# A recurrent attention fed into a PReLU network: one hand-written order of instructions replaced by another

## Chip, cores and metric

The kernel runs on one core of a Trainium2 chip. The metric is the device time of one execution in microseconds (us), as the median of several. The engines are TensorE (PE; its weight loads are listed as PEld), VectorE (DVE), ScalarE (ACT) and GpSimd (POOL); SyncE (SP) issues transfers (DMA), and ACT and POOL issue some too.

## The reference

Four batches of eight heads have 768 positions of 48 numbers. A recurrence gives y, which is laid out as 3072 tokens of 384 numbers and passed through a network with 2048 hidden units:

```python
f = 1.0 / (1.0 + np.exp(-f_logit))
state = np.zeros((B, H, D, D))
for t in range(S):
    state = f[:, :, t, :, None] * state + np.einsum('bhd,bhe->bhde', k[:, :, t], v[:, :, t])
    y[:, :, t] = np.einsum('bhd,bhde->bhe', q[:, :, t], state)
x = y.transpose(0, 2, 1, 3).reshape(B * S, H * D)
h = x @ w_in
g = np.maximum(h, 0.0) + alpha * np.minimum(h, 0.0)
return g @ w_out
```

## The kernel before

**Steps.** The sequence is cut into 6 chunks of 128 positions, and the batches into 2 pairs. This makes 12 steps, numbered 0 to 11, each of 256 tokens. A step has an attention part, whose result is a tile xT (384 x 256), and a network part, which turns xT into 256 rows of the output.

**Attention part.** It loads f, q, k, v (L313, L323; by SP in step 0 and by POOL in the others), takes the sigmoid (ACT), and forms products of decays on DVE (L338, L373 to L406, L440). PE then runs small products, mostly 48 x 32 weights, 64 instructions to a group: raw (L582) for lags of 0 to 3 positions, qu (L591) for lags inside a block of 32, off (L566) between blocks. DVE picks from them what counts (L599, L451) into a tile ad, ACT places that in A (L606), and PE multiplies with v and the state (py, L614), whose result ACT copies out (L494, in steps 0 and 1 L729). The keys are turned, by PE (pk, L713) in steps 0 and 1 and through DRAM (SP, L473 and L475) later, and the increments of the state (pd, L539, 64 products) are added by DVE (L550, L554). The result y goes to DRAM and back into xT by SP (L503, L505), or token by token (L626) in steps 1 and 11, or over PE (L738) in step 0.

**Network part.** Layer 1 makes eight pieces ph of the hidden units (L831). A piece is 6 products in full float32 (each two records), or, for pieces 3 to 6 from step 3 on, three passes in a faster form: xh with hi, xl with lo, xs with sum. xl and xs come from an accumulating DMA that POOL issues (L823). ACT makes the negative part (relu, L854), DVE two products that make the gate (L859). Layer 2 of step 0 is a plain product (po, L866). From step 1 on, it is seven block products in the manner of Strassen (pa twice, pc, pb, pd, pe, pf; L886, 16 records each), for which DVE adds halves of the gate (L880, eight per step, named m, u, v, w) and combines the results (L896, ACT L921); SP stores them (L765).

**Weights.** w_in and w_out come as float64 words, in eight pieces each of about 767 KB (L277, SP), and are cut to float32 by two ACT operations (L281, L282) and one of DVE (L291). That runs beside the first two steps. Fourteen idle products (L935) stand at the start of PE's work, six more before the first small products, and eight behind them.

**What sets the order.** `ORDER_WORDS` names every part of the work once, for instance `0u1` (step 0, qu of batch 1) or `3Na5` (network of step 3, layer-1 piece 5). Letters used below: e loads, G the two scans (L373, L374), r raw, u qu, o off, d increments, y py (of batch 0 or 1 of the pair, the two halves of one PSUM tile), Y the copy of py out of PSUM (ACT, L494, L729), I and J the filling products of step 0, K the way of the keys, X the way of y into xT; in networks a, b the products of a piece, r and c its relu and gate, p0 to p6 the block products (pa, pc, pb, pa, pd, pe, pf), u, v, w, m the sums, s the stores; without a step's number a and w are the two halves of converting a w_in piece, b and v those of w_out. The loop at the end (L947 to L959) calls the parts in the order of the words, and each engine under the manual schedule gets its instructions in that order. Those engines are PE, DVE and ACT; what SP and POOL issue is ordered by the framework.

Of the kernel before, what the change touches and what calls it, by code (L numbers as in the profile page):

```python
# [18 lines left out]
C = 128  # L19
# [22 lines left out]
0e 1e 0I0 0f 0F 0G 0g 0r1 0h 0i 0m 0p 0j 0r0 0I1 0l 0I2 a0 0R0 0I3 0I4 0I5 0q 0o a1 0k a2 0O 0s 0t w0 0u0 0U0 0R1  # L42
0K0 0H0 1f 0J0 0J1 0J2 w1 0K1 0u1 0J3 0U1 1F 0A0 0d 0D 0H1 0A1 w2 1G 0J4 0J5 0y0 0Y0 b0 0J6 0y1 0x0 0Y1 0M 1g 1i 0J7
1r0 0x1 1R0 0X a3 1h a4 b1 w3 a5 1m 1r1 w4 1j 0Na0 v0 0Nr0 0Na1 0Na2 1R1 0Na3 a6 0Nc0 w5 0Nr1 0Na4 0Na5 0Nc1 2e 0Nr2
1l 1k 0Nr3 a7 0Nc2 1o b2 0Nr4 1K0 1p 1O v1 w6 w7 0Na7 1K1 0Nc3 0Nc4 b3 v2 b4 0Na6 1q 0Nr5 0Nc5 1u0 0Nr6 b5 0Nc6 0Nr7
v3 1u1 1s 2f 1U0 0Nc7 b6 1U1 1H0 1A0 2F 1t 0Np0 v4 0Np1 0Np2 v5 1d b7 v6 V 1H1 1D v7 2g 0Np3 0Np4 1A1 1y0 1y1 1Y0
0Np5 W0 1Y1 1X W1 Y3 W2 0Np6 W3 2G 1Na0 W4 W5 0Np7 0No0 2h 1M 0No1 2i 1Nr0 1Na1 Y4 Y5 1Na3 2p 1Nr1 2q W6 1Na2 1Na4
Y6 3e 1Nr2 2u0 2l 1Nc0 1Nr3 2t 1Nc1 2k 1Nm0 1Nr4 1Nc2 2r0 1Nc3 W7 1Nm1 1Na5 1Nc4 1Na6 1Nr5 2R0 1Nr6 2r1 2U0 2K Z3
2u1 1Nc6 2R1 2A0 1Na7 1Nr7 1Nc5 2o 1Np0 2U1 2O 3f 1Nc7 2d Z4 1Nk 2D 2A1 1Np2 3F 1Np1 2y0 2y1 1Np3 2Y0 2Y1 2X 1Nu0
1Nu1 1Nv0 3G 3g 1Np4 1Nd 1Nv1 1Nw0 1Ng 2M 1Nw1 1Ne 1Nj 1Nh 1Np5 3h 1Np6 1Nf 1Nl 3p 1Ni 3i 1NL 2Na0 3l 4e 2Nr0 2Na1  # L50
2Nr1 2Na3 2Na2 1Ns1 3q 2Nr2 3r0 3u0 2Nc0 2Nr3 3k 3t 2Nc1 2Nm0 3R0 3U0 2Na5 2Nc2 2Nc3 2Nm1 2Na4 Z5 2Nr4 3r1 2Nr5 3K
3u1 2Na7 3R1 2Na6 3o 3A0 2Nc5 2Nr6 2Nc4 3O 3U1 2Nc6 Z6 3A1 3d 3D 2Np0 2Nr7 2Np1 2Nk 2Nc7 4f 2Nd T 3y0 3y1 4F 3Y0
2Np2 1Ns0 3Y1 3M 4g 2Np3 4r0 2Nu1 2Nu0 2Np4 3X 2Nv0 4G 2Nv1 2Nw0 2Ng 3Nx 3Ny 2Nw1 2Ne 2Nj 2Nh 2Np5 4h 2Np6 2Nf 2Nl
4p 3Na1 3Nz 3Na0 4i 3Nr0 2NL 2Ni 4k 4l 3NY 3Na2 4q 3Nr1 3Na7 4K 3Na3 5e 2Ns1 3Nr2 3Nc0 3NZ 3Na4 3Nc2 4t 3Nc1 3Nr7
3Nm0 4u0 3Nc7 4R0 4U0 3Nq3 3Na6 4r1 4A0 4R1 3Na5 4u1 4U1 3Nq4 3Nq5 3Nq6 4o 4O 3Nb3 3Nr3 3Nc3 3Nb4 3Nm1 2Ns0 3Nb6
3Nb5 4d 3Nr4 3Nr5 4D 3Np0 4A1 3Nr6 3Nc6 3Nc5 4y0 3Nc4 4y1 3Np2 5f 4M 4Y0 4Y1 3Np1 3Nk 5F 4X 5g 3Np3 3Nu0 3Nu1 3Nv0
5G 3Nv1 3Nw0 3Ng 3Np4 4Nx 4Ny 3Nw1 3Nd 3Ne 5h 3Nj 3Np5 3Np6 3Nh 3Nf 3Nl 5p 3Ni 5r0 4Nz 4Na0 5i 4Nr0 4Na1 3NL 5k 4NY
4Na5 5l 4Nq5 4Na2 5q 4Nr1 5K 4Na3 4Nc0 4Nr2 5u0 5t 4Nc1 4Nm0 4Nc2 5R0 5U0 4Na7 4Nr7 4NZ 4Na4 6e 3Ns1 5r1 4Nc7 4Nq4
4Nq3 5A0 5u1 5R1 5U1 4Na6 4Nb5 4Nb3 5o 4Nq6 4Nr3 5d 5O 4Nc3 4Nb4 5A1 4Nm1 5D 4Nr4 4Nr5 4Nb6 4Np0 4Nr6 5y0 4Nc4 4Nc5
6f 4Nc6 5y1 5Y0 6F 4Np2 5Y1 5X 6g 4Nk 4Np1 4Np3 4Nu0 4Nu1 4Nv0 4Nv1 4Ng 6G 5Nx 5M 4Nw0 4Np4 5Ny 4Nw1 4Nd 3Ns0 4Ne 6h  # L60
4Nj 4Nh 4Np5 4Nf 4Nl 6p 4Ni 5Nz 5Na0 4Np6 6i 5NY 6k 5Nr0 5Na1 4NL 6l 5Na2 6q 5Na7 5Nr1 6t 5Nc1 6u0 5Nr2 5Nc0 6r0
5Nm0 5Nc2 6R0 5Nr7 5NZ 7e 4Ns1 5Na4 6K 5Na3 6U0 5Nc7 5Na5 6r1 5Nq3 6A0 6u1 6R1 6U1 5Nq4 5Nb3 5Nq5 5Na6 5Nb4 6o 5Nr3
5Nq6 5Nc3 6O 6A1 6d 5Nm1 5Nb6 6D 5Nb5 5Nr4 5Nr5 5Np0 5Nr6 5Nc4 5Nc6 7f 6y0 5Nc5 5Nk 7F 6y1 6Y0 5Np2 6Y1 5Np1 6X 7g
5Np3 5Nu0 5Ng 7G 5Nu1 5Nv0 5Nv1 5Nw1 5Np4 6Nx 5Nw0 5Nd 6M 5Ne 6Ny 7h 5Nj 5Nh 5Np5 5Nf 5Np6 4Ns0 7p 5Ni 6Nz 6Na0 5Nl
7i 7l 6NY 6Nr0 6Na1 5NL 7k 7q 6Na2 6Nr1 7t 6Nc1 6Nr2 6Nc0 6Na7 6Nm0 7K 6Na3 6Nq3 7r0 6Nc2 7u0 7R0 6Nr7 6NZ 6Na4 8e
5Ns1 7U0 6Nc7 6Nq4 6Na5 7u1 7r1 6Nq5 7A0 7R1 7U1 6Na6 6Nq6 6Nb3 6Nr3 6Nc3 6Nb4 6Nm1 6Nb6 6Nb5 7A1 7o 6Nr4 6Nr5 6Nc4
6Nr6 7d 8f 6Np0 7O 6Nc5 7D 6Nk 6Np1 7y0 8F 7y1 6Nc6 7Y0 6Np2 7Y1 7X 8g 7Nx 7M 6Np3 6Nu0 6Nu1 6Np4 6Nv0 6Nd 6Nv1 6Nw0
6Ng 8G 7Ny 6Ne 6Nj 6Nw1 8h 6Nh 6Np5 6Nf 7NY 6Np6 5Ns0 6Nl 8p 6Ni 8i 7Nz 7Na0 7Nr0 7Na1 7Nr1 6NL 8k 8l 7Na2 8t 8r0
7Nr2 7Nc0 8q 7Nc1 8R0 9e 6Ns1 8K 7Na3 7Nm0 7Na7 8u0 7Nc2 7Nr7 7NZ 7Na4 8U0 7Na5 7Nq3 7Nq4 7Nc7 8r1 8u1 7Nq5 8A0 7Na6
8R1 7Nb4 7Nb3 8U1 7Nq6 7Nr3 7Nc3 7Nm1 7Nb6 7Nb5 8o 8A1 8d 7Nr4 7Nr5 7Nc4 7Nr6 8D 8O 9f 7Np0 7Nc5 7Nk 7Np1 7Nc6 8y0  # L70
9F 8y1 8Y0 8Y1 7Np2 8X 9g 7Nd 8M 7Np3 7Nu0 7Nu1 8Nx 7Ne 7Np4 7Nv1 7Ng 9G 8Ny 7Nv0 7Nw0 7Nw1 7Np5 7Nh 9h 7Nf 7Nj 9r0
7Np6 6Ns0 7Nl 9p 7Ni 9R0 8Nz 8Na0 8Na7 9i 8Nr0 8Na1 7NL 9k 9l 8Na2 9q 8Nr1 8NY 8Nr2 9t 8Nc0 8Nc2 8Nc1 8Nr7 8NZ 8Na4
10e 7Ns1 8Nm0 9u0 9U0 9K 8Na3 8Na5 8Nq4 9A0 8Nq3 9u1 9r1 8Na6 8Nc7 9R1 9U1 8Nq5 8Nq6 8Nb3 8Nb4 8Nr3 8Nc3 8Nm1 8Nb6
8Nb5 8Nr5 9o 8Nr4 8Nc5 9A1 8Nr6 9O 9d 8Np0 8Nc4 9D 8Nk 8Np1 8Nc6 10f 9y0 9y1 8Np2 10F 9Y0 9Y1 9X 10g 9M 8Np3 8Nu0
8Nu1 10r0 8Np4 8Nd 9Nx 8Nv0 8Nv1 8Nw0 8Ng 10G 8Np5 8Ne 8Nw1 9Nz 10h 9Ny 8Nh 8Nj 8Nf 10p 8Np6 7Ns0 8Nl 8Ni 9NY 9Na0
# [21 lines left out]
ORDER = flat()  # L97


@with_exitstack  # L100
def kernel(
# [147 lines left out]
    def load_weights(dst, src, name):  # L249
# [25 lines left out]
        def upper(n):  # L275
            raw = stage.tile([128, WP, 4], I16, tag="raw", name=f"{name}_raw{n}", bufs=RAWS)
            nc.sync.dma_start(out=raw.rearrange("p (a n) four -> p a (n four)", a=rows_)[:, :, 0:4 * width - 1],  # L277
                              in_=words[:, :, 4 * n * width + 1:4 * (n + 1) * width])

            lead = stage.tile([128, WP], F16, tag="lead", name=f"{name}_lead{n}", bufs=LEADS)  # L280
            nc.scalar.activation(lead, raw[:, :, 2].bitcast(BF16), AF.Copy, scale=0.5)  # L281
            nc.scalar.activation(as_int(n, I32), by_row(raw.bitcast(U32)[:, :, 0]), AF.Copy, scale=2.0 ** -13)  # L282
            got[n] = lead
# [21 lines left out]
    def loaded(bp, c, x):  # L305

        i = f"{bp}_{c}"
        b0 = U * bp
        loads = nc.gpsimd if bp or c else nc.sync

        def load(name, src):
            t = work.tile([128, W], F32, tag=name, name=f"{name}_{i}", bufs=1)
            loads.dma_start(out=t.rearrange("p (u x) -> p u x", u=U),  # L313
                              in_=src[b0:b0 + U, c].rearrange("u p h t -> p u (h t)"))
            return t

        x["kt"] = load("f", fT)
        f = x["f"] = quads(x["kt"])
        q = x["q"] = load("q", qT)
        x["k"] = load("k", kT)  # L320
        for cc in range(NC2):
            t_, _ = halves(cc)
            loads.dma_start(out=vs[bp][t_, cc, :, 0:DM], in_=v[b0:b0 + U, c, t_].rearrange("u t d -> t u d"))  # L323

    def lagging(bp, c, x):
        f, q = x["f"], x["q"]
        x["k4"] = work.tile([128, W], F32, tag="k4", name=f"k4_{bp}_{c}", bufs=1)
        kr = quads(x["k4"])
        nc.scalar.activation(f, f, AF.Sigmoid)
        nc.scalar.copy(kr[:, :, 2:3], f[:, :, 3:4])  # L330
        nc.scalar.copy(qd[:, :, 0:DB], q.rearrange("p (g t) -> p g t", t=DB))

    def lagged_all(bp, c, x):
# [7 lines left out]
        nc.vector.tensor_tensor(kr[:, :, 1:2], f[:, :, 2:3], f[:, :, 3:4], ALU.mult)  # L341
        lagged(1)
        nc.vector.tensor_tensor(kr[:, :, 0:1], f[:, :, 1:2], kr[:, :, 1:2], ALU.mult)
        lagged(2)
# [670 lines left out]
```

## Time and profile before

| what | value |
|---|---|
| median of 3 runs | 595.64 us (595.24 to 597.02) |
| span of the profiled execution | 592.1 us (592.08) |
| time of the profiled execution itself | not recorded apart from its span |
| instructions | 18,853 |
| first layer-1 product to last block product | 42.70 to 588.62 us |
| k, q, f loads from step 1 on | 512 KB each, 4.2 to 5.2 us to landing |
| weight pieces | 16 of about 767 KB, 9.5 us to landing |

The span goes from the first to the last record of the profile; the median is 3.56 us longer. An engine's busy time is the time in which one of its instructions runs. A wait is idle time of an engine ahead of an instruction, put down to what released it; "issue" means that the profile shows nothing that was waited for. The granted clock is the share of its full speed that PE got.

### The profile page before, as it was taken

Reading aid. Unit: us, or ns where it says so; the run is one execution under the profiler, and the core shown is the slowest. Engines: PE = TensorE matmul, PEld = TensorE weight load, DVE = VectorE, ACT = ScalarE, POOL = GpSimd, SP = SyncE. Lnnn points to the kernel's source line nnn. Section 1 sums busy time; section 2 is a strip of 40 time slices with the busy share of each in tenths; the row PEclk is TensorE's granted clock in tenths of the full one; section 3 lists DMA queues with packets and bytes.
Section 4 is the critical chain, followed back from the end, with each engine's and each line's share of the span. In section 5 each row is a group of like instructions: output and inputs, shape, how many; then the busy total and the mean of one; then the engine's idle time right before and its main releaser. Section 6 shows DMA issues by size and latency. Waiting matters only on the chain.

```text
span 592.1 us, 18853 instructions
## 1 busy us (share of the span) xinstructions
PE 580.1 (98%) x8200; PEld 527.9 (89%) x8200; DVE 505.7 (85%) x1027; ACT 300.4 (51%) x561; POOL 68.4 (12%) x114
## 2 busy tenths in 40 slices
PE   8799999999999999999999999999999999999997
PEld 6678767899899999999999999899899999899997
DVE  7889799899999989899989889989989979966243
ACT  5697973461472473483382374374275355443230
POOL 9110010000101101111111101101100100100100
PEclk9689999999999999999999999999999999999999
DMA  9959212612523823724624614722732731611300
GB/s 299 356 160 348 98 22 63 172 30 86 123 86 91 191 78 89 172 65 105 169 60 106 153 68 106 164 74 85 148 110 81 152 110 54 112 44 30 80 2 27
DMA packets 69443, 67.57 MB, mean 114 GB/s; under 512 B 44688, under 2 KB 58640, under 8 KB 69360
## 3 DMA queue, kind: packets, MB, share of 16 engines
q1 hardware_dynamic: 59744, 37.16, 22.1%
q0 software_dynamic: 8880, 28.84, 19.2%
q8 instruction: 64, 1.05, 0.7%
q10 hardware_dynamic: 736, 0.37, 0.2%
q14 instruction: 19, 0.16, 0.1%
HBM read 44.99 MB, written 13.50 MB: 99 GB/s over the span
## 4 chain that ended last, share of the span: by engine, by line
PE 80%; issue 10%; DMA 4%; ACT 3%; DVE 3%; POOL 1%; POOLq 0%; ACTq 0%; DVEq 0%
PE ph L831 36%; PE pa L886 9%; PE pd L886 5%; PE pf L886 5%; PE pe L886 5%; PE pb L886 5%; PE pc L886 4%; PE py L614 3%; PE qu L591 3%; PE raw L582 3%; DMA w_out_raw<-in_w_out 2%; PE pd L539 1%; PE off L566 1%; DVE ad L451 1%; DMA f<-in_fT 1%
## 5 line engine op out<-in xcount | busy, mean ns | idle before, releaser
L831 PE MATMUL ph<-xT,w_in_sb 128*128 128x256 f32 x612 | 137.1, 380 | 0.2 <-DMA xT<-y 0.2
L831 PEld LDWEIGHTS ph<-xT,w_in_sb 128*128 128x128 f32 x612 | 115.1, 190 | 16.9 <-issue 0.9
L854 ACT ACTIVATE gate<-ph 128x512 f32<-128x512 f32 x96 | 54.6, 594 | 134.4 <-PE ph L831 127.5
L859 DVE SCALAR_TENSOR_TENSOR gate<-gate,om,ph 128x256 f32<-128x256 f32 x192 | 81.0, 476 | 25.6 <-ACT gate L854 25.1
L886 PE MATMUL pa<-w_out_sb,gate 128*128 128x192 f32 x352 | 61.7, 329 | 0.0
L880 DVE TENSOR_TENSOR gate<-gate 128x512 f32<-128x512 f32 x88 | 57.6, 690 | 3.2 <-PE pb L886 2.4
L886 PEld LDWEIGHTS pa<-w_out_sb,gate 128*128 128x128 f32 x352 | 57.1, 190 | 0.5
L599 DVE COPY_PREDICATED ad<-mraw,raw 128x256 f32<-128x256 int32 (+1 forms) x96 | 42.7, 445 | 8.9 <-PE raw L582 6.2
L451 DVE COPY_PREDICATED ad<-mquad,qu 128x224 f32<-128x224 int32 (+6 forms) x140 | 42.2, 302 | 6.8 <-PE qu L591 1.7
L606 ACT COPY A<-ad 32x256 f32<-32x256 f32 x96 | 38.7, 403 | 11.8 <-DVE ad L451 10.4
L440 DVE TENSOR_TENSOR scores<-scores,fs 128x768 f32<-128x768 f32 (+5 forms) x60 | 37.4, 623 | 1.6
L844 ACT ACTIVATE ph<-ph 128x512 f32<-128x512 f32 x36 | 20.2, 574 | 34.0 <-PE ph L831 25.2
L831 PE MATMUL ph<-xh,hi 128*128 128x256 f32 x216 | 34.4, 295 | 0.0
L831 PE MATMUL ph<-xl,lo 128*128 128x256 f32 x216 | 32.0, 283 | 0.3 <-issue 0.3
L886 PE MATMUL pb<-t,gate 128*128 128x192 f32 x176 | 31.2, 331 | 0.0
L831 PEld LDWEIGHTS ph<-xh,hi 128*128 128x128 f32 x216 | 28.7, 190 | 2.8 <-issue 1.6
L424 ACT COPY A<-q 48x512 f32<-48x512 f32 x44 | 27.2, 617 | 7.8 <-DVE q L398 7.2
L886 PE MATMUL pd<-t,gate 128*128 128x192 f32 x176 | 30.7, 328 | 0.3 <-DVE gate L880 0.3
L886 PE MATMUL pc<-t,gate 128*128 128x192 f32 x176 | 30.6, 327 | 0.0
L886 PE MATMUL pf<-w_out_sb,gate 128*128 128x192 f32 x176 | 30.5, 327 | 0.0
L323 POOL DMA_DIRECT2D vs<-in_v x22 | 13.2, 605 | 149.4 <-PE py L614 149.1
L886 PE MATMUL pe<-w_out_sb,gate 128*128 128x192 f32 x176 | 30.4, 326 | 0.0
(153 smaller groups left out, 1044.0 us busy)
## 6 DMA issues: line engine op xcount, KB each, us to landing
w_out_raw<-in_w_out SPq DMA_DIRECT2D x8, 767.8 KB, 9.6
w_in_raw<-in_w_in SPq DMA_DIRECT2D x8, 767.2 KB, 9.5
q<-in_qT POOLq DMA_DIRECT2D x11, 512.0 KB, 5.1
f<-in_fT POOLq DMA_DIRECT2D x11, 512.0 KB, 5.2
k<-in_kT POOLq DMA_DIRECT2D x11, 512.0 KB, 4.2
turned<-f SPq DMA_DIRECT2D x40, 128.0 KB, 4.4
ksn<-turned SPq DMA_DIRECT2D x10, 512.0 KB, 3.5
out<-o SPq DMA_DIRECT2D x24, 192.0 KB, 1.9
```

Source lines behind the costliest of these rows:

```text
L424: nc.scalar.copy(A[halves(cc)[1], :, par * HP:(par + 1) * HP, CH * cc:CH * (cc + 1)], x["q3"][rows(par)].rearrange("p (u h c) s t -> p u h ...
L440: nc.vector.tensor_tensor(by_four(us[:, :, UO[m]:UO[m] + 4 * n]), by_four(us[:, :, skip:skip + 4 * n]), spread(fq[:, :, 1:1 + n], n), ALU. ...
L451: nc.vector.copy_predicated(ad[:, u, :, :, 4 * m:DB], mquad[:, lo:lo + n].bitcast(I32).unsqueeze(1).unsqueeze(1).broadcast_to((128, 2, HP, ...
L582: nc.tensor.matmul(raw[DB * j:DB * (j + 1), par, hp * C:hp * C + QW], lhsT=x["k"][r_, g * DB:(g + 1) * DB], rhs=qd[r_, g], start=True, sto ...
L599: nc.vector.copy_predicated(adu[:, :, :, d:4], mraw[:, d, :, d:4].bitcast(I32).unsqueeze(1).broadcast_to((128, H, NB, n)), rv[:, :, QO[d]: ...
L606: nc.scalar.copy(A[s_, u, :, s_], ad[s_, u].rearrange("p r h t -> p (r h) t"))
L831: nc.tensor.matmul(banks[f][:, j * T:(j + 1) * T], lhsT=of[:, kt, 128 * j:128 * (j + 1)], rhs=by[:, kt], start=first_ and kt + j == 0, sto ...
L844: nc.scalar.activation(banks[f], banks[f], AF.Copy, scale=1.0 - 1.0 / EPS)
L854: nc.scalar.activation(to, of, AF.Relu, scale=-1.0)
L859: nc.vector.scalar_tensor_tensor(to[:, j], to[:, j], om[:, m:m + 1], of[:, j], ALU.mult, ALU.add)
L880: nc.vector.tensor_tensor(block(to)[:, p], block(x_)[:, p], block(y_)[:, p], op)
L886: nc.tensor.matmul(banks[to][:, 0:DH], lhsT=block(of)[:, f], rhs=of_w_out(by)[:, f], start=start and f == 0, stop=f == NH - 1, skip_group_ ...
```

## The change

The words become finer and are put in another order, for all engines. Each part becomes a generator that stops (`yield`) after an instruction or a group, and each occurrence of its word runs it to the next stop. So one part can be spread: `0F 0F 0F a1 1ev 0ek` runs three instructions of F, then a stage of a weight piece, then two loads. The word e is split into ef, eq, ek, ev. POOL and SP are put under the manual order, so the place of a word sets when their transfers are issued as well. Tiles that more than one part needs are made at first use (`Later`). The instructions are the same; a tile pd_ is renamed inc_. The lines move: py to L717, ph to L944, the block products to L1002, the gate to L968 and L975, the sums to L996.

```diff
+class Later(dict):
+    def __init__(self):
+        self.make = {}
+    def __missing__(self, key):
+        self[key] = self.make[key]()
+        return self[key]
...
+class Word:
+    def __init__(self, part):
+        self.part, self.left = part, None
+    def __call__(self):
+        if self.left is None:
+            got = self.part()
+            self.left = got if hasattr(got, "gi_frame") else iter(())
+        next(self.left, None)
...
         def whole(f):
             banks[f] = bank(f"ph{f}_{i}")
             if by_parts(f):
                 products(f, late["hi"][:, f - SPLIT[0]], late["xh"], True, False)
+                yield
                 products(f, late["lo"][:, f - SPLIT[0]], late["xl"], False, False)
...
-    with tc.manual_schedule(engines={mybir.EngineType.PE, mybir.EngineType.DVE, mybir.EngineType.Activation}):
+    with tc.manual_schedule(engines={mybir.EngineType.PE, mybir.EngineType.DVE, mybir.EngineType.Activation,
+                                     mybir.EngineType.Pool, mybir.EngineType.SP}):
...
+        run = {key: Word(part) for key, part in run.items()}
         for key in ORDER:
             run[key]()
```

Some stretches of the words, as they were and as they are (the ends of step 1's and step 2's attention, and the last block products of step 9's network):

```diff
-1A1 1y0 1y1 1Y0 0Np5 W0 1Y1 1X W1 Y3 W2
+1A1 1A0 1A0 1A0 1A0 1y1 1Y1 1y0 1Y0 1X 1X 1X
...
-2y0 2y1 1Np3 2Y0 2Y1 2X
+2y1 2Y1 1Nu0 1Nv0 3h 2y0 2Y0 2X 2X
...
-9Np2 10y0 10M 9Nd 10y1 10Y0 10Y1 9Np3 9Ng 11G 10X 11g 9Nu1 9Nu0 9Nv0 9Np4 9Nv1 9Nw0 9Np5
+9Np2 9Nu0 10Y1 10Y0 11q 11R0 9Nm1 11q 9Np3 11h 11u0 11R0 11G 11i 11i 11i 11r1 11k 10X 10X 10X 9Nv0 11l 9Np1 11U0 9Nu1 9Nd 11U0 9Nv1 11k 11K 9Np4 9Np5 9Nw0
```

More of the change, by code (lines that the diff above doesn't have):

```diff
@@ L47 @@
[L47 to L51, printed above, removed]
@@ L315, in load, with f_, q_, k_ @@
             return t
[L317 to L323, printed above, removed]
+        def f_():
+            x["kt"] = load("f", fT)
+            x["f"] = quads(x["kt"])
+        def q_():
+            x["q"] = load("q", qT)
+        def k_():
+            x["k"] = load("k", kT)
+        def v_():
+            for cc in range(NC2):
+                t_, _ = halves(cc)
+                loads.dma_start(out=vs[bp][t_, cc, :, 0:DM], in_=v[b0:b0 + U, c, t_].rearrange("u t d -> t u d"))
+                if not cc:
+                    yield
+        return {"ef": f_, "eq": q_, "ek": k_, "ev": v_}
     def lagging(bp, c, x):
-        f, q = x["f"], x["q"]
+        f = x["f"]
         x["k4"] = work.tile([128, W], F32, tag="k4", name=f"k4_{bp}_{c}", bufs=1)
@@ L466, in fifth @@
             carried(x)
+            yield
             nc.vector.transpose(x["kt"], x["ks"].rearrange("p g s t -> p (g s t)"))
         def keys():
-            ksn = x["ksn"] = work.tile([128, U, HP * 128], F32, tag="ksn", name=f"ksn_{i}", bufs=1)
+            ksn = x["ksn"]
             way = dram.tile([128, W], F32, tag="turned", name=f"turned_{i}", bufs=2)
@@ L486, in out_ @@
         def out_(u):
-            if not u:
-                x["py"] = pair(f"py_{i}")
             summed(x["py"], bp, u)
         def kept_out(u):
-            if not u:
-                x["y"] = work.tile([128, HP, U, C], F32, tag="ksn", name=f"y_{i}", bufs=1)
             nc.scalar.copy(x["y"][:, :, u], x["py"][:, u].rearrange("p (h t) -> p h t", h=HP))
@@ L633, in opening @@
         i = f"{bp}_{c}"
+        ahead(bp, c, x)
         def two(name):
@@ L716, in kept_keys @@
         def kept_keys(u):
-            if not u:
-                x["ksn"] = work.tile([128, U, HP * 128], F32, tag="ksn", name=f"ksn_{i}", bufs=1)
             nc.scalar.copy(x["ksn"][:, u], x["pk"][u])
         def out_(u):
-            if not u:
-                x["py"] = pair(f"py_{i}")
             summed(x["py"], bp, u)
         def kept_out(u):
-            if not u:
-                x["y"] = work.tile([128, HP, U, C], F32, tag="ksn", name=f"y_{i}", bufs=1)
             nc.scalar.copy(x["y"][:, :, u], x["py"][:, u].rearrange("p (h t) -> p h t", h=HP))
         def dense_(u):
-            if not u:
-                x["xt"] = [bank(f"xt{kt}_{i}") for kt in range(NK)]
             for kt in range(NK):
@@ L956 @@
                 run.update({(f"J{k}", 0): lambda x=x: idled(x["off"][0], 256) for k in range(BEHIND)})
-        assert sorted(run, key=str) == sorted(ORDER, key=str), (set(run) ^ set(ORDER), len(ORDER) - len(set(ORDER)))
+        assert set(run) == set(ORDER), set(run) ^ set(ORDER)
+        run = {key: Word(part) for key, part in run.items()}
         for key in ORDER:
             run[key]()
+        assert all(word.ended() for word in run.values()), [key for key, word in run.items() if not word.ended()]
 def _level_masks():
```

232 lines of the change are left out of this document (164 added, 68 removed).

## The prediction

> **What bounds the kernel now.** First the page's span and busy times, then its slices:
>
> ```profile
> span 592.1 us, 18853 instructions
> ...
> PE 580.1 (98%) x8200; PEld 527.9 (89%) x8200; DVE 505.7 (85%) x1027; ACT 300.4 (51%) x561; POOL 68.4 (12%) x114
> ...
> PEclk9689999999999999999999999999999999999999
> ```
>
> TensorE (PE) is the bound; its granted clock dips in the second slice alone. The windows view gives stretches (length, busy time of PE, PEld, DVE, ACT, POOL, granted clock, DMA share, GB/s):
>
> ```profile
> 15.50:19.00 3.50, 0.99 (x66) 0.91 (x67) 3.44 (x9) 2.90 (x6) 1.89 (x3) 0.99 1.01 391
> 19.00:33.00 14.00, 14.00 (x244) 11.15 (x242) 11.51 (x26) 9.15 (x20) 0.73 (x1) 0.51 1.01 334
> 43.00:589.00 546.00, 543.99 (x7504) 498.58 (x7502) 471.25 (x966) 269.33 (x503) 50.47 (x69) 1.00 0.39 101
> ```
>
> The first layer-1 product (ph) starts at 42.70 us, the last block product ends at 588.62. From 43 to 589 PE idles 2.0 us. So an order of the same instructions can win little after 43 us, and whatever wait it adds to PE is lost one for one. The waits view from 42 to 593 us (total, times, longest) names what there is to win:
>
> ```profile
> PE off L566 <- issue: 0.7, 1, 0.7
> PE ph L831 <- issue: 0.3, 1, 0.3
> PE pd L886 <- DVE gate L880: 0.3, 1, 0.3
> PE ph L831 <- DMA xT<-y: 0.2, 1, 0.2
> ```
>
> Two have no data behind them: "issue". The DMA view from 206 to 209 us, around the larger (packets, MB, share of 16 engines):
>
> ```profile
> q0 software_dynamic: 158, 0.58, 75.2%
> q8 instruction: 1, 0.02, 2.0%
> ```
>
> q8 is PE's own code: the page has 64 packets of it, 1.05 MB, so 16 KB each, and 16,400 PE records over 64 packets are 256 instructions each. In the trace this packet ran from 206.25 to 207.21, while a k load held q0, and PE went on at 208.66, 1.45 us later. At the other wait the packet ended at 342.27 and PE went on at 343.70, 1.43 us later. Both times PE had just run small products, which use up code fastest (64 qu and 64 off last 1.7 us).
>
> **The change part by part.** Both kernels have the same instructions. Only orders change, SP's and POOL's included. I followed the new orders with their semaphore waits and added row durations between each wait and what releases it.
>
> (1) Small products apart. A packet starts 1.1 to 1.5 us after PE comes within 64 instructions of the block before it, 3.3 to 5.5 us beside a load; with 1.0 us of packet and 1.43 behind, 320 instructions must last about 3.7 us, or 5.6 beside a load. After the first ph ten such stretches of the old order are under 5.6 (the two that waited: 4.78 and 5.54), two of the new (5.27 and 5.38). Gain: 0.69 idle, and 0.61 at 343.70, where an xl group took 1.33 instead of 0.72: **-1.3** (ends -1.3 and 0).
>
> [...]
>
> (2) Time behind transfers. At 90.91 step 1's network waits for xT; twelve products take 3.33 us with the wait, 2.59 elsewhere. Between py of step 1 and its first ph lie 5.4 us of PE work in the old order, 12.5 in the new, and in no step under 11.6; the longest such transfers in the trace take 8 to 10. **-0.74.** xl and xs keep 20.1 and 26.1 us of cover, against 16.3 and 21.4 needed: nothing.
>
> (3) pd at 498.37 waits for DVE, where two scans (1.3 us) stand ahead of the sums; 16 products take 3.17 instead of 2.60. In the new order a second block product lies between pb and pd. **-0.57.**
>
> (4) The first large product behind small ones takes 2.80 us for 16, others 2.60. Such returns fall from 51 to 48: 3 x 0.20, **-0.6**; the sums of all PE rows (542.76 and 542.16) give the same.
>
> (5) The readout of py. py of the two batches are halves of one tile. In the new order the words of steps 1, 2, 4, 6, 7 and 8 read `1y1 1Y1 1y0`: the first half is copied out (Y, ACT) ahead of the other half's products (y), and PE's order then has a wait on ACT in front of these. In the old order both y come first (`1y0 1y1 1Y0`), except in step 0, whose price the timeline shows:
>
> ```profile
> 34.10 1.15 PE L614 MATMUL py<-A,vs 128*64 128x64 f32 x32 [0.78 <-ACT ad L688]
> 35.19 0.70 PE L935 MATMUL off_0a<-ones 128*128 128x256 f32 x2
> 35.78 0.58 ACT L729 COPY y<-py 128x512 f32<-128x512 f32 x1
> ...
> 36.42 1.15 PE L614 MATMUL py<-A,vs 128*64 128x64 f32 x32 [0.54 <-ACT y L729]
> ```
>
> The second group starts 0.06 us after the copy ends and had waited, with two filling products between. In the six steps PE has nothing between. With ACT free: 0.16 until a reader follows PE's last product, 0.59 of copy (0.587 in its row), 0.05 on: 0.80. 6 x 0.80, **+4.8**; in step 7 ACT has part of a relu ahead, **+0.3**. Ends: 0, if PE really waits for nothing there, and 9, if ACT has one relu (0.59) ahead each time.
>
> (6) DVE's lateness. DVE gets faster by the new order: in the trace a DVE instruction that needs the result of the one just ahead starts 0.034 us after its end, any other 0.083 before it; such direct successors fall from 316 to 187, 129 x 0.117 = 15 us. That doesn't shorten PE, and PE's waits on DVE stand closer: at the first qu of step 6 PE has one ph piece and pf (2.59 + 2.60) since the last gate it needed, DVE a combination (0.35), score products (some 2.6), three operations on the state (0.95, 0.55, 0.55), a raw copy (0.44) and gaps until the pair of banks is free: 5.7, late by 0.5. The same in step 5; six places more are late by 0.05 to 0.15 each, where ph or qu waits for a bank. Also pb directly behind the last ph in steps 1 and 2: its gate is ready 1.3 and 1.8 us after PE leaves ph (0.16, relu 0.59, DVE 0.48 twice), pb reads it at 1.95 and 2.27: nothing. **+1.8.** Ends: 0 and 7.6, one sum (0.69) late in each of 11 networks.
>
> (7) The start. pk (at 18.77) comes at about 15.9 by its rows, but the k load of step 0 stands behind a weight piece on SP, and more conversions lie ahead on ACT; the sums put the first ph 0.5 us later than the old order's. Then a ph piece waits 0.8 for a bank that DVE reads behind weight sums, and the increments of step 1 wait 1.7 for ACT's copy of the keys behind weight conversions. Together 3.0; weight landings (9.5 us in the median, 6 to 20 in the trace) may move all of it. **+2.0**; ends -2.7, the clock not halved, and +4.
>
> (8) SP's and POOL's other moved transfers are covered by 11 us and more of PE work (the two stores of network 0 ahead of the keys' way back: 25). The tail keeps its copy, store and 3.46 us. Nothing.
>
> Sum: 592.08 of the profiled span plus 3.56 around it is the median 595.64. 595.64 - 1.3 - 0.74 - 0.57 - 0.6 + 4.8 + 0.3 + 1.8 + 2.0 = **601.3**: slower. The same sums along the old order find its wait at pd and no other of over 0.1 from DVE or ACT.
>
> **The rivals.**
> (a) Only the readouts count: DVE and the start give nothing away. 592.43 + 4.8 = 597.2, at the bound of "no change". For: DVE's 15 us. Against: the chains of (6) and (7).
> (b) The other side: the six readouts cost nothing, because the waits are met when PE gets there. 592.4 with nothing lost elsewhere. It decides from 0.23 us per readout, above which the gain is under 0.3%. For: no such wait is seen after 42 us in the old kernel. Against: step 0's row.
> (c) DVE becomes the bound. It is busy 471 of 546 us; one more sum late per network makes (6) 7.6: 607.1.
> (d) The pause of PE near 15 us gets too short to halve the clock. In the trace PE was busy 0.99 of 3.50 us, then got 0.51 for 14.00 us of unbroken work; without that the first ph comes 2.7 earlier: 596.6 to 598.6. [...]
>
> **How the numbers follow.** 0.3% is 1.8 us, about what a measurement of this kernel can tell from no change. Forecast 0.52 (598.6 to 604; the fetch rule's 602.6 lies in it), (a) 0.13, (b) 0.08, (c) 0.17, (d) 0.10. Faster: (b) but for its upper edge, 0.07. Same (593.85 to 597.4): half of (a), half of (d) and the rest of (b), 0.13. Slower: 0.80. The range leaves out (b) and the far end of (c): 596.5 to 606.
>
> **What would show it.** PE's waits: py on ACT y (L717) six times, some 0.8 each; qu on DVE at steps 5 and 6; none for issue beside a k load, for xT, for pd. ph's first start near 43.2, with the clock row's second slice telling of (d). If PE doesn't wait at py, the sign is wrong; if waits on the gate (L975, L996) sum to over 5 us, it is (c).

## The result and the profile after

The kernel after takes **613.09 us** in the median of 4 runs (612.14 to 614.59); the kernel before, run beside it, 595.44 us (593.93 to 597.02, 4 runs). The ratio is 1.0299, with a 95% interval of 1.0274 to 1.0323. The forecast was 601.3 us: the sign was right, and of the 17.65 us lost only 5.66 were foreseen. The profiled execution took 612.78 us, with a span of 610.4. Its page has, in the rows known from before:

```profile
span 610.4 us, 18819 instructions
...
PE 586.5 (96%) x8200; PEld 531.0 (87%) x8200; DVE 493.6 (81%) x1027; ACT 303.3 (50%) x561; POOL 66.8 (11%) x114
...
PEclk9679999999999999999999999999999999999999
```

The same 8200 matmul records take 6.4 us longer, and DVE got 12.1 us faster (15 were forecast), which did not shorten PE's time. PE is still the bound, now with pauses. PE's ten largest waits from 43 to 612 us (total, times, longest):

```profile
PE py L717 <- ACT y L587: 3.6, 5, 0.9
PE ph L944 <- issue: 2.7, 3, 1.3
PE inc L633 <- ACT ad L802: 1.5, 1, 1.5
PE py L717 <- ACT A L709: 1.0, 2, 0.5
PE inc L633 <- ACT A L672: 1.0, 1, 1.0
PE py L717 <- ACT y L839: 0.7, 1, 0.7
PE qu L690 <- DVE scores L530: 0.5, 1, 0.5
PE qu L690 <- issue: 0.4, 1, 0.4
PE ph L944 <- DVE f L504: 0.4, 1, 0.4
PE qu L690 <- DVE ad L543: 0.3, 1, 0.3
```

Six of them are the readouts of py (five on L587, one on L839), as forecast. xT and pd are gone, as forecast. "Issue" wasn't to appear beside a load, and is here four times. The 1.5 ahead of inc (the increments, pd_ before) stands where (7) forecast 1.7; the 1.0, in step 7, was not forecast. The start is in the windows (length, busy time of PE, PEld, DVE, ACT, POOL, granted clock, DMA share, GB/s):

```profile
15.50:19.00 3.50, 1.92 (x72) 1.50 (x72) 3.47 (x10) 2.58 (x5) 1.89 (x3) 1.00 0.89 297
19.00:33.00 14.00, 12.49 (x234) 9.55 (x235) 6.76 (x19) 9.33 (x22) 1.73 (x3) 0.53 1.02 309
...
36.80:40.20 3.40, 3.40 (x25) 2.98 (x22) 3.16 (x5) 2.83 (x7) 0.00 (x0) 0.50 0.01 2
...
74.50:78.00 3.50, 3.50 (x68) 2.62 (x69) 3.41 (x8) 3.44 (x5) 0.00 (x0) 0.53 0.02 5
```

Before, the clock was halved once, from 18.9 to 32.6 us. Now it is halved there, although PE was busy for 1.92 of the 3.5 us ahead (0.99 before), and again at 36.8 and at 74.3. The first ph starts at 45.64 us instead of 42.70.

**Where the time went.** Up to the first ph 2.94 us are lost. Behind it I laid each group of PE beside the usual duration of such a group, its row. What is beyond the rows (a pause, and the slower products next to it) sums to 2.3 us in the kernel before and 18.4 after; the rows themselves sum to 0.6 less in the new order. 2.94 + 18.4 - 2.3 - 0.6 = 18.4, and the spans differ by 18.3. The 18.4 are: readouts 6.3 (five of 0.90 and 1.80 in step 7), waits for issue 4.5, the stretch from the first ph to 80 us 3.1, qu waiting for DVE in steps 5 and 6 1.2 (0.80 of it idle), inc of step 7 waiting for ACT 1.2, and 2.1 in small pieces. These shares shift by up to about 1 us with the duration that is taken as usual; the idle times and the total do not.

One readout, in step 2, in the timelines of PE and of ACT (start, duration, what, idle time before and its releaser):

```profile
135.06 1.15 PE L717 MATMUL py<-A,vs 128*64 128x64 f32 x32
136.90 1.15 PE L717 MATMUL py<-A,vs 128*64 128x64 f32 x32 [0.69 <-ACT y L587]
```

```profile
136.26 0.59 ACT L587 COPY y<-py 128x512 f32<-128x512 f32 x1 [2.56 <-PE py L717]
```

ACT had been idle for 2.56 us, so the copy starts as soon as the first half is there, and PE's second half starts 0.05 us behind the copy's end. This is the row of step 0 again, without filling products in between.

One wait for issue, in PE's timeline, and the DMA queues around its packet (packets, MB, share of 16 engines):

```profile
205.85 1.08 PE L690 MATMUL qu<-scores,k 48*32 48x112 f32 x64
206.91 0.91 PE L681 MATMUL raw<-qd,k 48*32 48x80 f32 x64
207.75 0.98 PE L944 MATMUL ph<-xh,hi 128*128 128x256 f32 x6
208.57 0.40 PE L944 MATMUL ph<-xl,lo 128*128 128x256 f32 x2
210.14 0.74 PE L944 MATMUL ph<-xl,lo 128*128 128x256 f32 x4 [1.18 <-issue]
```

```profile
q1 hardware_dynamic: 4132, 0.52, 71.8%
q0 software_dynamic: 21, 0.09, 19.6%
q8 instruction: 1, 0.02, 1.1%
```

Two small groups, qu and raw, stand end to end in the *new* order, although the change is meant to keep them apart; PE stops eight products of a large piece later, while its code (q8) shares the engines with 4132 small packets on q1. I counted PE's instructions in blocks of 256 and put beside each stop the packet that brings the block. Every stop comes at the same place of a block, to within one instruction (number 193 to 195 of 256, counted from PE's first record):

| kernel | PE within 64 instructions of the block before | packet | its end + 1.43 | PE goes on |
|---|---|---|---|---|
| before | 202.89 | 206.25 to 207.21 | 208.64 | 208.66 |
| after | 158.83 | 165.84 to 166.80 | 168.23 | 168.25 |
| after | 200.58 | 207.62 to 208.50 | 209.93 | 210.14 |
| after | 445.34 | 449.02 to 449.94 | 451.37 | 451.34 |
| after | 492.00 | 495.77 to 496.83 | 498.26 | 498.11 |

All four stops end within 0.21 us of their packet's end + 1.43, as the forecast has it. The packets start 7.01, 7.03, 3.68 and 3.78 us behind the second column, against 3.36 before: the two long stops have very late packets; the two short ones have packets about as late as before, and stretches of small products that end before 6 us.

### The profile page after: what moved, and what is told of

The parts are those of the page before. It is cut to its first block, busy times and chain, and to the rows that moved or that the text cites. A ratio compares the mean times of both kernels' runs of the same rounds, so it can differ in the third digit from the quotient of the medians.

```text
span 610.4 us, 18819 instructions
## 1 busy us (share of the span) xinstructions
PE 586.5 (96%) x8200; PEld 531.0 (87%) x8200; DVE 493.6 (81%) x1027; ACT 303.3 (50%) x561; POOL 66.8 (11%) x114
## 3 DMA queue, kind: packets, MB, share of 16 engines
q0 software_dynamic: 8880, 28.84, 18.3%
q8 instruction: 64, 1.05, 0.7%
## 4 chain that ended last, share of the span: by engine, by line
PE 63%; DVE 18%; ACT 7%; DMA 5%; issue 3%; SPq 1%; POOL 0%; DVEq 0%; ACTq 0%; POOLq 0%
PE ph L944 26%; PE pa L1002 7%; PE pb L1002 4%; PE pf L1002 3%; PE py L717 3%; PE pd L1002 3%; PE qu L690 3%; PE pc L1002 3%; PE pe L1002 3%; PE po L982 2%; DVE scores L530 2%; PE raw L681 2%; DVE ad L700 2%; DMA f<-in_fT 1%; DVE gate L996 1%
## 5 line engine op out<-in xcount | busy, mean ns | idle before, releaser
L944 PE MATMUL ph<-xT,w_in_sb 128*128 128x256 f32 x612 | 141.1, 382 | 1.6 <-issue 1.3
L944 PEld LDWEIGHTS ph<-xT,w_in_sb 128*128 128x128 f32 x612 | 113.6, 190 | 18.2 <-issue 2.6
L968 ACT ACTIVATE gate<-ph 128x512 f32<-128x512 f32 x96 | 56.0, 596 | 139.2 <-PE ph L944 106.5
L975 DVE SCALAR_TENSOR_TENSOR gate<-gate,om,ph 128x256 f32<-128x256 f32 x192 | 85.5, 476 | 41.8 <-ACT gate L968 41.3
L996 DVE TENSOR_TENSOR gate<-gate 128x512 f32<-128x512 f32 x88 | 59.9, 687 | 7.9 <-PE pb L1002 4.1
L1002 PE MATMUL pa<-w_out_sb,gate 128*128 128x192 f32 x352 | 61.7, 329 | 0.0
L1002 PEld LDWEIGHTS pa<-w_out_sb,gate 128*128 128x128 f32 x352 | 57.2, 190 | 0.8
L512 ACT COPY A<-q 48x512 f32<-48x512 f32 x44 | 27.1, 617 | 18.4 <-DVE q L482 17.7
L717 PE MATMUL py<-A,vs 128*64 128x64 f32 x768 | 27.5, 226 | 7.1 <-ACT y L587 3.6
L717 PEld LDWEIGHTS py<-A,vs 128*64 128x64 f32 x768 | 24.4, 138 | 11.2 <-ACT y L587 4.3
L944 PE MATMUL ph<-xh,hi 128*128 128x256 f32 x216 | 33.6, 295 | 0.0
L944 PE MATMUL ph<-xl,lo 128*128 128x256 f32 x216 | 32.1, 287 | 1.4 <-issue 1.4
L440 ACT COPY scores<-qd 128x256 f32<-128x256 f32 x48 | 29.2, 679 | 7.2 <-DVE qd L407 6.8
L407 DVE TENSOR_TENSOR qd<-qd,f 128x768 f32<-128x768 f32 (+2 forms) x36 | 27.3, 759 | 5.7 <-ACT qd L400 5.5
L944 PE MATMUL ph<-xs,sum 128*128 128x256 f32 x216 | 30.9, 289 | 0.3 <-ACT ph L958 0.3
L1002 PE MATMUL pb<-t,gate 128*128 128x192 f32 x176 | 30.9, 329 | 0.0
L1002 PE MATMUL pd<-t,gate 128*128 128x192 f32 x176 | 30.8, 328 | 0.0
L1002 PE MATMUL pc<-t,gate 128*128 128x192 f32 x176 | 30.7, 328 | 0.0
```

Source lines behind the costliest of these rows:

```text
L407: nc.vector.tensor_tensor(qdv[d], qdv[d - 1][:, :, :, 1:5 - d], f[:, :, 1:5 - d].rearrange("p (g i) r -> p g i r", i=NB), ALU.mult)
L440: nc.scalar.copy(x["q4"][:, :, :, r], qdv[r][:, :, :, 0])
L717: nc.tensor.matmul(py[64 * par:64 * par + 64, u, o:o + CH], lhsT=vs[bp][:, cc, u, hd * D:hd * D + 64], rhs=A[:, u, par * HP + hp, CH * cc: ...
L944: nc.tensor.matmul(banks[f][:, j * T:(j + 1) * T], lhsT=of[:, kt, 128 * j:128 * (j + 1)], rhs=by[:, kt], start=first_ and kt + j == 0, sto ...
L968: nc.scalar.activation(to, of, AF.Relu, scale=-1.0)
L975: nc.vector.scalar_tensor_tensor(to[:, j], to[:, j], om[:, m:m + 1], of[:, j], ALU.mult, ALU.add)
```

## The experiments

The theory: four things cost the time, each in its own place (readouts, start, waits for code, DVE's and ACT's lateness). Rivals: the fixed order of SP and POOL; the clock; DVE as the bound.

**1. The readouts out of the new order** (the same in steps 4, 6, 7 and 8):

```diff
-1y1 1Y1 1y0 1Y0
+1y1 1y0 1Y1 1Y0
...
-2y1 2Y1 1Nu0 1Nv0 3h 2y0 2Y0
+2y1 1Nu0 1Nv0 3h 2y0 2Y1 2Y0
```

> The changed kernel with one thing put back: in steps 1, 2, 4, 6, 7 and 8 the copy-out of py's first half (Y) again stands behind the second half's products. Theory (the six readouts are lost one for one, because PE has nothing to run meanwhile): the six waits of py on ACT y vanish; with them go 0.90 us each in five steps and 1.80 in step 7, 6.3 us in all, so 613.1 becomes 606.8 (606 to 608.5). Rival (DVE and ACT are late anyway, and PE waits at the next product instead): 611.5 or more, with new waits of the block products, inc or ph behind the readouts.

608.01 us (ratio to the kernel before 1.0207, 1.0180 to 1.0235), 5.1 less than the kernel after. In its waits no py waits for a copy y; new is

```profile
PE pa L1002 <- ACT o L1033: 0.9, 1, 0.9
```

That is within the expected range, and less than the 6.3 of the rows, because a part comes back elsewhere: pa now waits 0.92 for a combination on ACT, and the waits for issue, at other counts of time, are 4.8 instead of 3.2. The wait of inc in step 7 is gone with the readouts.

**2. The readouts into the old order**, and nothing else (`1y0 1y1 1Y0` becomes `1y0 1Y0 1y1`, and so in steps 2, 4, 6, 7 and 8):

> The old kernel with one part of the change alone: in steps 1, 2, 4, 6, 7 and 8 the copy-out of py's first half stands ahead of the second half's products. Theory (each readout is lost one for one, 0.80 to 0.90 us, with part of a copy of pa ahead of it on ACT in step 6): six waits of py on ACT y, 5.3 us in all, 600.8 (600 to 601.8). Rival (some of it is taken back, since PE's pause lets DVE and ACT catch up and so removes waits of the old kernel): 598 to 600.

600.75 us (1.0095, 1.0064 to 1.0125), as expected: 5.07 more than the kernel before beside it.

```profile
PE py L613 <- ACT y L493: 4.6, 5, 1.8
PE off L565 <- issue: 1.3, 1, 1.3
PE py L613 <- ACT y L728: 0.7, 1, 0.7
```

Six waits: five of 0.69 to 0.71, and one of 1.83, where ACT has other work ahead of the copy. Step (5) is confirmed from both sides.

**3. SP and POOL back to the framework:**

```diff
-    with tc.manual_schedule(engines={mybir.EngineType.PE, mybir.EngineType.DVE, mybir.EngineType.Activation,
-                                     mybir.EngineType.Pool, mybir.EngineType.SP}):
+    with tc.manual_schedule(engines={mybir.EngineType.PE, mybir.EngineType.DVE, mybir.EngineType.Activation}):
```

> The changed kernel with SP and POOL left to the framework again; the words and so PE, DVE and ACT are as in the changed kernel. Theory (PE's code packets come late because the words bunch POOL's loads of f, k, q, v and SP's stores: four to six transfers in flight, packets 4 to 10 us late): loads spread out, issue waits after the first ph fall from 3.5 us of idle time in six places to 1.5 or less; 610 (607 to 611.5). Rival (the small products of PE's new order alone make the issue waits): they stay, 612 to 614. Transfers that come at other times may add a wait for data of their own, to be read from the waits.

615.54 us (1.0339, 1.0301 to 1.0377). The idle time at issue falls from 3.2 to 2.4 us, but the first ph comes at 48.4, 2.8 later than in the kernel after, and a wait for turned keys is added (0.67). The time lies above what either theory expected. Giving the order of SP and POOL back wins nothing as a whole; whether it would behind the start, this run doesn't separate.

**4. The old words, with SP and POOL bound to them** (a load at the place of its old word):

> The old order of words in the changed kernel's program: every part runs all its pieces at its old place, and the four loads of a step are issued together at the place of the old word e; SP and POOL follow the words. PE, DVE and ACT have the old kernel's orders. Theory (what SP and POOL issue in the order of words bunches transfers and lets them wait for one another): 597 to 602, with issue waits or waits for loads that the old kernel doesn't have. Rival (SP's and POOL's order costs nothing, the loss is all in the order on PE, DVE and ACT): 595.5, within 1 us.

647.15 us (1.0865, 1.0836 to 1.0895), far above what either theory expected.

```profile
PE pd L1001 <- DVE gate L995: 20.2, 3, 8.9
PE ph L943 <- DMA xs<-xl: 11.6, 2, 6.5
```

In the kernel before, the framework places the transfers, so the old words were not made for them. Bound to the places of these words they come late (11.6 us of waits for xs), and the work behind them with them. Which of the bound transfers costs what isn't separated here.

**5. Shifting PE's code.** 32 products of 32 x 32 whose result nobody uses (128 instructions) ahead of the idle products:

```diff
+        for _ in range(32):
+            nc.tensor.matmul(idle[0:32, 0:32], lhsT=ones[:, 0:32], rhs=ones[:, 0:32], start=True, stop=True)
```

> The changed kernel with 32 products of 32 x 32 more ahead of the idle products at the start, where PE waits for the first loads anyway: they add 128 PE instructions, so every boundary of 256 instructions falls half a block earlier in the work. Nothing else changes. Theory (issue waits are PE's code arriving late): the four waits at a ph piece (168 us), an xl pass (210), a qu (451) and an xl pass (498) leave these products, and others may come at new places near the same bunches of transfers; their sum after the first ph lies anywhere from 0.5 to 6 us, the time at 610 to 616. Rival (they are data waits that the profile doesn't name): they stay at the same products, 613.

621.26 us (1.0414, 1.0372 to 1.0457). No wait for issue is left at its product; there are four others, at 361.98, 414.45, 458.54 and 496.62 us (1.40, 1.16, 2.67, 0.99), of products that had not waited. No data ties them, only the count. Each ends within 0.15 us of a packet's end + 1.43. The time is above the 610 to 616 expected, and isn't a measure of the shift alone, since the first ph came at 49.55.

**6. More transfers beside the old order.** A copy of q (512 KB) to a place that nobody reads, after each load; PE, DVE and ACT keep their instructions:

```diff
+        if c:
+            spare = dram.tile([128, W], F32, tag="spare", name=f"spare_{i}", bufs=2)
+            nc.gpsimd.dma_start(out=spare, in_=q)
```

> The old kernel, in which from chunk 1 on each q, once loaded, is copied from its tile to a scratch place in DRAM that nobody reads: 512 KB more beside the loads of f and k, at the time of step's small products (an earlier run's copies came all at the start and told nothing). Theory (packets of PE code wait behind transfers in flight, so more of these make more issue waits in an unchanged order of PE): issue waits after the first ph rise from 1.0 us to 2.5 or more, 597 to 601. Rival (the packets' lateness doesn't depend on them): 595 to 596, waits as before. A load of f or k that comes later by POOL's wait for q may add up to 1 us of its own, to be told from the waits.

599.15 us (1.0063, 1.0045 to 1.0082). PE's timeline and a window behind it:

```profile
343.87 0.28 PE L834 MATMUL ph<-xl,lo 128*128 128x256 f32 x1
346.43 1.43 PE L834 MATMUL ph<-xl,lo 128*128 128x256 f32 x5 [2.29 <-issue]
```

```profile
346.40:350.00 3.60, 3.57 (x18) 3.57 (x19) 1.03 (x5) 1.37 (x3) 0.00 (x0) 0.55 0.19 66
```

The wait that was 0.35 us is now 2.29 (the packet ran from 344.11 to 345.04, and 345.04 + 1.43 = 346.47), the one at 208.66 rose from 0.69 to 1.43, and the clock was halved for 3.4 us (346.22 to 349.63) at the longer. The packet of 343 started 5.69 us late instead of 3.71. So with the copies in flight this packet of PE's code came 1.98 us later.

An earlier form of it read f twice instead:

```diff
+            loads.dma_start(out=spare.rearrange("p (u x) -> p u x", u=U), in_=fT[b0:b0 + U, c].rearrange("u p h t -> p u (h t)"))
```

> The old kernel, with one transfer more from chunk 1 on: beside each load of f, the same 512 KB are copied from DRAM to a scratch place in DRAM that nobody reads. No engine's work on data changes. Theory (PE's code packets queue behind whatever is in flight, so bunched transfers make issue waits whatever PE's order is): the packets' mean delay rises from 2.5 us to 3 or more, issue waits after the first ph rise from 1.0 us to 3 or more; 598 to 602. Rival (short stretches of small products alone decide): issue waits stay at 1 to 1.5 us, 595.5 to 596.5.

594.73 us (0.9992, 0.9979 to 1.0006). It tells nothing: the copies wait for no buffer, and the framework issued all ten by 41 us.

**7. Small groups taken apart in the new order** (with the readouts of experiment 1): off of steps 3 and 9, raw of step 4 and inc of steps 9 and 10 moved behind a large piece, for instance

```diff
-9u0 7Ns1 9o 8Nq3 8Nc1 8Nc1 9U0 9U0 9l 9O 8Nq4 8Na7 9O
+9u0 7Ns1 8Nq3 8Nc1 8Nc1 9U0 9U0 9l 8Nq4 8Na7 9o 9O 9O
```

> The changed kernel with the six readouts mended as in the first experiment, and five pairs of small groups taken apart: off of step 3 behind the ph piece that followed it, raw of step 4 and the increments of steps 9 and 10 behind both passes of the piece that followed, off of step 9 behind the ph piece that followed. Theory (two small groups in a row use up a block of 256 PE instructions in 1.7 us, faster than the next packet can come; that is where the issue waits of the changed kernel stand): the issue waits near 167, 209, 447 and 495 us, 4.8 us of idle time in the kernel with mended readouts, fall to 1.5 or less; 608.0 becomes 604.5 (603.5 to 606). Rival (transfers in flight alone decide, and nearly every block meets some): the waits stay or move, 607 or more.

613.38 us (1.0291, 1.0251 to 1.0330) instead of the 604.5 expected: the waits for issue fall from 4.8 to 0.8, as the theory has it, but the time rises by 5.4 over experiment 1.

```profile
PE ph L944 <- DVE gate L975: 3.9, 3, 2.3
...
PE ph L944 <- DMA xs<-xl: 0.7, 1, 0.7
PE raw L681 <- issue: 0.6, 1, 0.6
```

As I read it, in a fixed order DVE waits for the moved products and comes late with the gates behind them; no run shows this by itself. At the longest of these waits, and at that of inc at 74.6, the clock was halved too (from 452.55 for 3.4 us and from 73.67 for 6.8). Keeping small products apart is possible here, but it seems that the instructions of the other engines must move with them.

**8. The old start.** The old order of all engines up to `0Na0`, then the new:

> The changed kernel, but all words up to the first layer-1 piece of step 1 stand in the old order (the rest follows in the new one). Theory (the start is a loss of its own: first ph 2.9 us later, PE's clock halved a second time near 38 us in a pause that waits for ACT's copies, then 3.2 us of waits for weights, banks and the increments of step 1 until 80 us): first ph back at 42.7 to 43.5, no such waits, 613.1 becomes 607 (605.5 to 609). Rival (what the start wins is waited for later, because DVE and ACT carry the same work either way): 611 or more, with new waits between 90 and 200 us.

609.07 us (1.0220, 1.0195 to 1.0245), 4.0 less than the kernel after and just above the 605.5 to 609 expected. First ph at 43.25, and no wait for inc at 74. The seam, where the two orders meet, has a price: raw waits 2.26 for DVE at 97, and a wait for issue of 1.93 is new at 213.27. That agrees with a start worth about 6 (2.94 + 3.1 by the rows), but only 4 of it are measured.

**9. Old start and mended readouts together:**

> The old order up to the first layer-1 piece of step 1, then the new one, with the six copy-outs of py behind both halves. Theory (start and readouts are separate and add up): 613.1 less 6 and less 5.1 is 602 (600 to 604); what stays above the old kernel is then issue waits (3 to 5 us) and waits of qu for banks. Rival (they share their cause, a late ACT): 605 or more.

608.73 us (1.0217, 1.0185 to 1.0250): no less than either alone, against 602 expected. The largest part of the difference stands in one place:

```profile
209.02 0.55 PE L662 MATMUL off<-q,kh 48*32 48x32 f32 x33
212.04 0.64 PE L662 MATMUL off<-q,kh 48*32 48x32 f32 x29 [2.46 <-issue]
```

The packet starts 8.87 us late (209.72 to 210.82; 210.82 + 1.43 = 212.25). The clock is 0.50 from 211.17 to 218.00. Some 6.5 us go between 200 and 225. The rival's number (605 or more) came out, but not its reason, a late ACT: no data holds this product back.

**10. The same with its code shifted** by nine 32 x 32 products (36 instructions) ahead of step 0's first ph, which the piece then overwrites:

```diff
+            if not n_ and not f:
+                for _ in range(9):
+                    nc.tensor.matmul(banks[f][0:32, 0:32], lhsT=ones[:, 0:32], rhs=ones[:, 0:32], start=True, stop=True)
```

> The kernel with the old start and mended readouts (608.7), with nine products of 32 x 32 more ahead of step 0's first layer-1 product: 36 PE instructions, so that later blocks of code end elsewhere in the work. Nothing else changes; the products cost 0.4 us. Theory (of its 13 us above the old kernel 6.5 us come from one block that ends at step 4's off at 212 us, its packet 6 us late behind loads of k, f, v and an xs transfer; the 2.5 us of pause then halve PE's clock from 211 to 218 us): that wait leaves this place, the clock stays at 1.0 there, 602.5 (601 to 605) unless another place gets as long a wait. Rival (step 4 itself is late on ACT or DVE, and PE would wait there for data): 607 to 609, with the same loss between 200 and 225 us.

605.78 us (1.0173, 1.0130 to 1.0217), 3 less than experiment 9, but above the 601 to 605 expected. The wait at 212 is gone and the clock there is full; 2.20 came at 164.6 and 1.45 at 489.6. So 36 instructions more moved the stop to other groups; 1.98 us more of delay beside added transfers (experiment 6) made one longer, 2.29 instead of 0.35.

**11. The start's clock.** Six idle products ahead of step 0's first py, to fill its pause:

```diff
+            if not bp and not u:
+                for _ in range(6):
+                    idled(x["off"][0], 256)
```

> The changed kernel with six idle products more ahead of step 0's first py, where PE waits 1.6 us for ACT's copies into A. Theory (that pause halves PE's clock a second time, from about 37 to 40 us): the clock stays at 1.0 after its return near 33 us, the first ph starts 1 to 1.7 us earlier than the changed kernel's 45.6, and the kernel takes 611 to 612. Rival (the start is bound by ACT and DVE, not by the clock): first ph at 45.6 or later, 613 to 614.

613.47 us (1.0307, 1.0267 to 1.0347).

```profile
33.00:42.00 9.00, 8.85 (x96) 6.96 (x94) 5.88 (x8) 7.98 (x17) 0.00 (x0) 0.96 0.25 60
```

The halving at 36.8 is gone, and the first ph comes 0.43 us earlier, not 1 to 1.7. So it makes only a small part of the late start. ACT and DVE, for which PE waits there (below), are left as the cause; no run shows that directly.

**12. What the forecast named, mended in the old order.** Three moves: the first piece of step 1 behind the last product of network 0 (for xT), the scans of step 11 behind the sums (for pd), and off of step 4 behind a large piece:

```diff
-2G 1Na0 W4 W5 0Np7 0No0
+2G W4 W5 0Np7 1Na0 0No0
...
-10Y1 9Np3 9Ng 11G 10X 11g 9Nu1 9Nu0
+10Y1 9Np3 9Ng 10X 11g 9Nu1 9Nu0 11G
...
-3Nq6 4o 4O 3Nb3
+3Nq6 3Nb3 4o 4O
```

> The old kernel with three words moved: step 1's first layer-1 piece behind one more pair of layer-2 products of step 0, step 11's two scans behind the u sums of network 9, and step 4's off and its copy behind a third pass of a piece. Theory (each removes one of the four waits of the old kernel without another change): 0.7 for xT, 0.5 for pd, 0.5 at the issue wait at 208: 593.8 (593 to 594.8), ratio 0.997. Rival (one of them moves to the next product): 595.0 to 596.

593.50 us (0.9958, 0.9943 to 0.9972, 8 runs). One wait is left between 43 us and the end:

```profile
PE ph L830 <- issue: 1.4, 1, 1.4
```

xT, pd and the stop at 208 are gone; the stop at 343 grew from 0.35 to 1.36. This kernel beats both. With raw of step 7 also behind a large piece (`7r1 7R1` behind `6Na6`):

> The old kernel with the three words moved as before (593.5 measured), and raw of step 7 taken from its place directly behind qu to behind a further ph piece, with its copies. Theory (the 1.36 us issue wait at 343 us is left by this pair of small groups): it goes, 592.2 (591.5 to 593). Rival (the packet is late anyway): 593.5.

593.74 us (0.9966, 0.9948 to 0.9984, 12 runs): the last wait for issue goes, 0.38 for a gate comes, and the time can't be told from the one above; the 592.2 expected did not come.

## Why the prediction was right in sign and wrong in size

| step | forecast | found |
|---|---|---|
| (1) code | -1.3 | 4.5 - 1.3 = +3.2 |
| (2), (3) xT, pd | -1.31 | -1.31 |
| (4) returns | -0.6 | -0.6 |
| (5) readouts | +5.1 | +6.3 |
| (6) DVE | +1.8 | +1.2, and 1.2 at inc of step 7 |
| (7) start | +2.0 | 2.94 + 3.1 = +6.0 |
| small pieces | 0 | +2.1 |

The third column sums to 18.1 of the span's 18.3 us. The forecast of 601.3 missed mainly by two steps: (1), the waits for PE's code, by 4.5 us, and (7), the start, by 4.0. Smaller parts are (5), by 1.2, the wait of inc in step 7 for ACT, 1.2, and the small pieces, 2.1; the last two stood at nothing in the sum. The 3.56 us that the sum adds around the span do not all lie outside it: where a time and its span are both known, they differ by 1.7 to 2.4 us, so the execution profiled before was faster than the median. The forecast starts from the median and is not moved by this.

**(1) failed.** The 1.43 held: every wait for issue over 0.4 us behind the first ph, in the kernel after and in the eleven experiments in which I counted, ends within 0.25 us of a packet's end + 1.43. The size failed, in two ways. The step says that 320 instructions must last "5.6 beside a load"; its own numbers (a packet up to 5.5 us late, 1.0 long, 1.43 behind it) give 7.9, and I had taken the low end. And packets come later than that: at 168.25 and 210.14 they started 7.0 us late, and the stretches lasted 8.1 and 8.4 us and were still too short. The old trace already had such a packet, 7.1 us late at 50.8 us beside weight loads, where no small products stood; the step left it out. Behind the first ph, 2 of 58 packets were over 5.5 us late before and 6 of 59 after, while the median moved only from 2.15 to 2.34. Short stretches became fewer, as counted (ten to two); the few very late packets became more. That the new order bunches the transfers is the likely reason: with the framework's order of SP and POOL (experiment 2) 3 of 59 are so late, and in experiment 6, with added transfers, a packet started 5.69 us late instead of 3.71. Behind the first ph, 4 of 59 blocks stop PE after the change (2 of 58 before); the stops leave 3.2 us of pauses after and 1.0 before. The 602.6 that stands with the chances is the forecast's sum with (1) at nothing; no run shows that term, and what the runs showed in its place are these stops.

**(2), (3) right.** Both waits are gone after, and experiment 12 takes them from the old kernel, 1.9 us together with the stop at 208.

**(4)** The row sums moved as said. No run tests it alone.

**(5) right in mechanism, a little small.** 0.90 a time instead of 0.80 in five steps. Step 7 was mis-sized: not 0.80 + 0.3 but 1.80, as the first half's products also wait for a copy of A (0.50; another 0.54 ahead of them is among the small pieces).

**(6) right in place for DVE**: qu waits at steps 5 and 6, where 0.5 each was forecast (0.48 and 0.32 idle). The six further places of 0.05 to 0.15 are too short to stand on the list of waits, and with them the step's own terms give 1.3 to 1.9, so 1.8 was at their upper end. What was missed is ACT: inc of step 7 waits 0.97 for a copy of A. I had followed DVE's order through every step and ACT's only at the readouts and the start.

**(7) mis-sized by three.** The wait ahead of inc was forecast as 1.7 and is 1.50, but the nearness is in part luck: the copy of the keys, which the step had PE wait for, ended at 70.50, and PE waits until 74.47 for four copies out of qu's banks (L802, 73.37 to 74.41), behind a weight conversion on ACT. From 74.34 the clock was halved for 3.41 us, which costs about as much again (1.7, an estimate: half of the 3.41) and stood at nothing in the sum, and the wait of ph for a bank is 0.43 instead of 0.8. The first ph is 2.94 late instead of 0.5: in the start PE waits 1.47 for a copy of A ahead of py, 1.15 for another, 1.0 for qu's scores (the waits view from 19 to 43 us), where the kernel before had waits of 0.8, 0.5 and 0.5. Cutting the sum from 3.0 to 2.0 because landings may move it was a guess in the wrong direction.

**The rivals.** (b) is out by the six waits. (a) had these right and is out by the start, which gave 2.94 away up to the first ph, and by the waits for code. (c) is out in mechanism: PE's waits on gates are nil, and DVE is busy 465 of 569 us. (d) is out: the clock was halved at the start as before, though PE had worked for 1.92 of 3.5 us, and twice more.

**Open.** With old start, mended readouts and shifted code (experiment 10) 10.1 us remain over the old kernel. Its pauses behind the first ph explain 7.4 of these (8.9 us against 1.5; the largest are raw 2.31, off 2.20, ph 1.45, pa 0.92), its halved clock from 99.04 to 102.45 some 1.7 (half of the 3.41, an estimate); the rest, about 1, is not placed. Also open is what in the transfers delays a packet most, their bytes or their number: at 205.5 to 210.5 the queue had thousands of small ones, in experiment 6 large ones.

## What to carry to other kernels

When an order is replaced and one engine is the bound, follow the queues of all the others, the quiet ones too: six copies on ACT ahead of the products that had stood before them cost PE 5.07 us here (experiment 2). Where PE runs a few hundred small products within few microseconds, look at when its next block of code lands and what is in flight beside it: here the stops rose from 1.0 to 3.2 us although short stretches fell from ten to two. Four words moved in the old order, for three waits that the profile named, gave 0.42% (interval 0.28 to 0.57%); 2167 words in a new order lost 2.99% (2.74 to 3.23%).

## What the runs showed of the hardware

**The clock behind short pauses.** In the kernel before, a quiet stretch near 15 us (PE busy 0.99 of 3.50 us) was followed by half clock from 18.94 us on. Here single pauses went with it: 1.50 us at 74.47, 2.29 in experiment 6, 2.46 in experiment 9, 2.67 in experiment 5. But 2.29 us at 96.72 in experiment 9 and 2.20 at 164.63 in experiment 10 were followed by full clock. The wait of raw for DVE came out both ways: 2.31 us at 97.50 in experiment 10 was followed by half clock from 99.04 to 102.45, and 2.26 us at 97 in experiment 8 by full clock. So the length of a pause alone doesn't settle it, and what does was not shown.

In the kernel after, the clock was halved from 19.73 us for 13.65, from 36.80 for 3.41 and from 74.34 for 3.41; these starts lie 17.07 and 37.54 us apart, 5 and 11 times 3.41. In the kernel before, it was halved for 13.65 us, with PE busy throughout (14.00 of 14.00 us from 19 to 33).

**Code beside transfers.** In the kernel after, behind the first ph, a packet of PE's code started 1.05 us or more after PE came within 64 instructions of the block before (0.93 in the kernel before; counted from 32 instructions instead of 64, some packets started up to 2.19 us ahead of the mark). Where the DMA engines were less than 10% busy meanwhile, half of the packets started within 1.3 us (the latest after 5.0); where they were over 30% busy, half started after 3.3 us or more. In experiment 9 one came 8.87 us late.
